# Rows of the last eight modes split in six and two; Z of the last two as four partial products; x of the first tile summed in PSUM

## The chip, the cores and the metric

The kernel runs on one core of one Trainium2 chip. The metric is the device time in microseconds (us), the median of three runs. All names of lines below (L432 and so on) are lines of the kernel before; the same lines of the changed kernel have higher numbers.

## The reference

Linear attention is followed by a spectral mixing block. With `phi(t) = elu(t) + 1`, batch 8, 8 heads, 576 positions and a head width of 64:

```
kv  = einsum('bhsd,bhse->bhde', phi(k), v);  z = phi(k).sum(axis=2)
x   = einsum('bhsd,bhde->bhse', phi(q), kv) / (einsum('bhsd,bhd->bhs', phi(q), z)[..., None] + 1e-6)
x   = x.transpose(0, 2, 1, 3).reshape(8, 576, 512)
X   = rfft(x, axis=1)[:, :64]                       # 64 modes are kept
Y   = einsum('bmd,mde->bme', X, w_r + 1j * w_i)     # one 512 x 512 complex matrix for each mode
u   = x + irfft(Y, n=576, axis=1)
out = u + relu(u @ w_ch)                            # 8 x 576 x 512 float32
```

The weights `w_r` and `w_i` are 64 matrices each of 512 x 512 in float32, together 134 MB to be read.

## The kernel before

**Stages.** First, q, k and v are loaded and x is formed and transformed by a product with DFT columns. Then `mode_pair(p)` runs for p = 0 to 30, two modes at a time: POOL issues the DMAs of the weights (`w_load`, L117, two buffers that alternate), TensorE multiplies the spectrum with them (`product`, L432, into `P`), `evacuate` copies `P` to SBUF, and `picks` (L455) adds the four column groups and puts Y, with the channels on partitions, into the PSUM tile `yt_ps`. While the weights of a pair land, TensorE does other work out of the list `work` (attention rows, the channel product of x, inverse transforms of the modes that are done), dealt out by `slots`, and `keep_warm(n)` (L419) adds n products of 128x512 whose result nobody reads. The inverse transform is a product too: `inv_sb` holds its rows, and `inv2_sb` and `lead_sb` hold such rows picked and reordered for the late modes.

**The last pair of modes.** `last_pair()` loads mode 62 and mode 63 in pieces (`w_load_last`, L129). Mode 62 goes through `product`, `evacuate` and `picks`. Mode 63 is computed turned, with the weights as the stationary operand (L513, `y_last`, 32 products of 128x16), in five pieces `PIECES` as the last weights land, eight or four products a piece, and one `keep_warm` product after some. The result of the eight last modes (56 to 63) is in `Y8` (128 channels x 4 x 8 modes x 16): seven modes are copied there by L506, the last one by L519.

**The tail.** From `Y8` two things are needed, with the 128 rows (mode, part, batch) on partitions: the rows themselves (half 0 of the tile `last`, by four transposes, L932) and Z, which is the rows times `w_ch` (half 1 of `last`, by products with `wch16`, L938). L933 and L934 copy the transposed rows to `last`, L943 copies Z. Two DMAs (L947, one on SP's queue, one on POOL's) send `last` to `YZ_all`, where the later batches read it. The output tiles are 128 x 512; two of them, a pair n, share `accs[n]` of two PSUM banks. For a tile the order is: `channels` (L800, the product of x with `w_ch`, kept in `E0`, is put in PSUM), `add_inverse(n, 1)` (L760, the inverse transform of Z is added), relu on ScalarE (L958 for single tiles, L810 later), `add_inverse(n, 0)` (the inverse transform of the rows is added), and one sum on VectorE that adds x out of SBUF (L962 for one tile, L834 for a pair), and then a store on SP's queue. The first eight tiles (pairs 0 to 3, batches 0 and 1) read `last` itself; later ones read `YZ_all`. The first tile is done apart: the inverse transform of its rows goes to `y0` (L944), VectorE adds it to x (L945), and one instruction does relu and sum (L973).

**What sets the order.** Nearly all instructions are pinned to the order of the program on their engine; each engine takes its own in that order. Semaphore waits follow from the tiles that are read and written, and from the reuse of buffers: `psW` has the tags "P" (two buffers), "yt" (one) and "zl" (one, the target of `keep_warm`), and after its release the pool `psT1` takes its banks for the accumulators of pairs 2 and 3.

Of the kernel before, what the change touches and what calls it, by code (L numbers as in the profile page):

```python
# [10 lines left out]
F32 = mybir.dt.float32  # L11
F16 = mybir.dt.float16
# [31 lines left out]
def kernel(  # L44
# [22 lines left out]
    NL = 8  # L67
    NE = NM - NL
    NF = NM // 2

    fwd_np, inv_np, pick_np = _dft_consts(S, NM)
    id16_dr = nc.inline_tensor(np.eye(128, dtype=np.float16), name="ident16")
# [343 lines left out]
    def keep_warm(n: int):  # L416

        for _ in range(n):
            pin(nc.tensor.matmul(last_ps[0], id16, wch16[:, 0, :]))  # L419
# [67 lines left out]
    def last_pair():  # L487
        xl = ystage.tile([128, NDL, 2 * B], BF16, name="xl")
        for h in range(2):
            src = xt_v[:, (2 * h + 1) * NDC : (2 * h + 2) * NDC, :, :, LAST]  # L490
            pin(
                nc.vector.tensor_copy(
                    out=xl[:, h * NDC : h * NDC + NDC], in_=src.rearrange("p c t b -> p c (t b)")
                )
            )
        w = w_get(LAST)
        kk = NM - 2
        work_slot(LAST, "start")
        P = psW.tile([128, D], F32, tag="P", bufs=2, name=f"P{kk}")
        for dc in range(NDL):  # L500
            n = 32 if dc < NDC else 2 * B
            product(P, xt_cols(dc, kk, n), n, w, dc, NDL)
        st = evacuate(kk, P)
        work_slot(LAST, "mid")
        picks(kk, st, 1)
        pin(nc.vector.tensor_copy(out=Y8[:, :, 0 : NL - 1, :], in_=yt_ps[:, :, 0 : NL - 1, :]))  # L506
        keep_warm(3)
        y_last = psW.tile([128, NDC, 2 * B], F32, tag="P", bufs=2, name="y_last")
        for piece in PIECES:
            for dc in range(piece.start, piece.stop):  # L510
                for ec in range(NDC):
                    pin(
                        nc.tensor.matmul(  # L513
                            y_last[:, ec, :], w[:, NDL + dc, ec * 128 : ec * 128 + 128], xl[:, dc, :],
                            start=(dc == 0 and ec == 0), stop=(dc == NDL - 1), skip_group_check=True,
                        )
                    )
            keep_warm(WARM[piece.stop])
        nc.vector.tensor_copy(out=Y8[:, :, NL - 1, :], in_=y_last)  # L519
# [18 lines left out]
    inv2_sb = ystage.tile([128, S], F16, name="inv2_sb")  # L538
    N_LEAD = 2
    lead_sb = [ystage.tile([128, S], F16, name=f"lead{b}_sb") for b in range(N_LEAD)]  # L540
    nc.sync.dma_start(out=inv_sb, in_=inv_dr.ap())
    YE_T = ystage.tile([128, NDC, NF, 2 * B], F16, name="YE_T")
    YL = [ystage.tile([128, NDC // 2, 2, 2 * NL, NF // NL, B], F16, name="YL0")]
# [62 lines left out]

    last_ps = []

    sel = sW.tile([128, 1 + N_LEAD, 128], F16, tag="rows", bufs=1, name="row_sel")

    def row_sets():
        pin(nc.vector.memset(sel, 0.0))
        for h in range(2):
            for g in range(NF // NL):
                r0 = 2 * NF + 2 * NL * ((g - 1) % (NF // NL))
                pin(
                    nc.vector.tensor_copy(
                        out=sel[:, 0, h * 64 + g : h * 64 + 64 : NF // NL], in_=id16[:, r0 : r0 + 2 * NL]
                    )
                )  # L620
        for b in range(N_LEAD):
            pin(nc.vector.tensor_copy(out=sel[:, 1 + b, b:128:B], in_=id16[:, 2 * NE : 128]))

    def row_set(i: int):
        dst = ([inv2_sb] + lead_sb)[i]
        for cols in (slice(0, 512), slice(512, S)):
# [157 lines left out]
    def on_bank(n: int, banks: set, ins):  # L784
        pin(ins)
        for other, theirs in users.setdefault(n, []):
            if not banks & theirs:
                tc.declare_no_dep(ins.ins, other.ins, reason="the other bank of the pair")
        users[n].append((ins, banks))
    accs: dict[int, object] = {}  # L790

    def channels(n: int, tiles_of=(0, 1)):
        if n not in accs:
            accs[n] = acc_pools[n % 4 // 2].tile([128, 2, D], F32, tag="acc", bufs=2, name=f"acc{n}")
        for i in tiles_of:
            t = pairs[n][i]
            for cols, src in e0_parts(t):
                on_bank(
                    n, {i},
                    nc.tensor.matmul(  # L800
                        accs[n][:, i, cols], id16, src, start=(cols.start == 0), stop=False,
                        skip_group_check=True,
                    ),
                )
# [94 lines left out]
    rows_work = [row_sets] + [lambda i=i: row_set(i) for i in range(1 + N_LEAD)]  # L899
# [8 lines left out]
    for p in range(n_early, LAST):  # L908
        mode_pair(p)
    assert not work  # L910
    psB.release()
# [3 lines left out]
    slots[LAST, "start"] = slots[LAST, "mid"] = N_PRE  # L915
    for n in range(N_PRE):
        work += [lambda n=n: channels(n), lambda n=n: first_rows(n)]
    last_pair()


    last = sW.tile([128, 2, D], F16, tag="rows", bufs=1, name="last")
    z1_ps = psW.tile([128, NDC, 8, 2 * B], F32, tag="yt", bufs=1, name="z1l")
    y_ps = [
        psW.tile([128, NDC, 128], F16, tag="P", bufs=2, name=f"ypl{h}")[:, 0 : NDC // 2] for h in range(2)
    ]
    y0 = psW.tile([128, D], F32, tag="P", bufs=2, name="y0l")
    last_ps.append(z1_ps.rearrange("p c m n -> p (c m n)"))
    rows = [Y8[:, ec].rearrange("p m n -> p (m n)") for ec in range(NDC)]
    hw = D // 2
    COLS = [slice(h * hw, h * hw + hw) for h in range(2)]  # L930
    for ec in range(NDC):
        pin(nc.tensor.transpose(y_ps[ec // 2][:, ec % 2, :], rows[ec], id16))  # L932
    pin(nc.scalar.copy(out=last[:, 0, COLS[0]], in_=y_ps[0].rearrange("p c r -> p (c r)")))  # L933
    pin(nc.vector.tensor_copy(out=last[:, 0, COLS[1]], in_=y_ps[1].rearrange("p c r -> p (c r)")))  # L934
    for h in range(2):
        for ec in range(NDC):
            pin(
                nc.tensor.matmul(  # L938
                    last_ps[h][:, 0:hw], rows[ec], wch16[:, ec, COLS[h]],
                    start=(ec == 0), stop=(ec == NDC - 1),  # L940
                )
            )
        pin(nc.scalar.copy(out=last[:, 1, COLS[h]], in_=last_ps[h][:, 0:hw]))  # L943
    pin(nc.tensor.matmul(y0, lead_sb[0][:, rows_of(0)], last[:, 0, :]))  # L944
    pin(nc.vector.tensor_tensor(out=x_of(0), in0=y0, in1=x_of(0), op=ALU.add))  # L945
    for h, eng in enumerate((nc.sync, nc.gpsimd)):
        eng.dma_start(  # L947
            out=YZ_all[64 * h : 64 * h + 64 : NF // NL].rearrange("r b z d -> r b (z d)"),
            in_=last.rearrange("p z d -> p (z d)"),
        )  # L950
    psW.release()
    acc_pools.append(
        tc.alloc_tile_pool(name="psT1", bufs=1, space=PSUM, side="left", reuse_waits="tile")
    )

    def relu(n: int, i: int):
        a = accs[n][:, i]
        on_bank(n, {i}, nc.scalar.activation(out=a, in_=a, func=AF.Relu))  # L958
# [8 lines left out]
        add_inverse(n, 1, (i,))  # L967
        relu(n, i)

    add_inverse(0, 1, (1, 0))  # L970
    on_bank(
        0, {0},
        nc.vector.scalar_tensor_tensor(  # L973
# [51 lines left out]
```

## Time and profile before

| | us |
|---|---|
| median of three runs (lowest, highest) | 421.56 (421.41, 422.10) |
| span of the profiled execution, first to last instruction | 419.4 |
| what lies around the span, median less span | 2.2 |
| TensorE busy in the span | 317.2 (76%) |
| VectorE busy in the span | 231.3 (55%) |
| ScalarE busy in the span | 154.2 (37%) |
| weights' queue (software DMA), share of the 16 DMA engines | 93.4% |
| last DVE instruction of mode 63's result (L519) ends at | 388.45 |
| first output store is issued at | 391.59 |
| last output store is issued at | 414.13 |

The runs are of whole executions; the profile is one execution, and its own time is the span and the 2.2 us around it. All places in time below are microseconds from the start of the span. A line of the timeline gives the start, the time until the group's last instruction ends, the engine, the line of the source, the operation, what it writes and reads, the shape and the count, and in brackets how long the engine stood idle before it and for whom. A line of the chain of waits gives the start, the length and what was at work. The ends of matmuls are modelled, and they overlap: ten of them that are listed with 2.32 us begin 0.215 us after each other.

### The profile page before, as it was taken

Reading aid. Unit: us, or ns where it says so; the run is one execution under the profiler, and the core shown is the slowest. Engines: PE = TensorE matmul, PEld = TensorE weight load, DVE = VectorE, ACT = ScalarE, POOL = GpSimd, SP = SyncE. Lnnn points to the kernel's source line nnn. Section 1 sums busy time; section 2 is a strip of 40 time slices with the busy share of each in tenths; the row PEclk is TensorE's granted clock in tenths of the full one; section 3 lists DMA queues with packets and bytes.
Section 4 is the critical chain, followed back from the end, with each engine's and each line's share of the span. In section 5 each row is a group of like instructions: output and inputs, shape, how many; then the busy total and the mean of one; then the engine's idle time right before and its main releaser. Section 6 shows DMA issues by size and latency. Waiting matters only on the chain.

```text
span 419.4 us, 7466 instructions
## 1 busy us (share of the span) xinstructions
PE 317.2 (76%) x3143; PEld 164.4 (39%) x3143; DVE 231.3 (55%) x509; ACT 154.2 (37%) x253; POOL 57.4 (14%) x100
## 2 busy tenths in 40 slices
PE   0369998999617875676767686988798877998993
PEld 0257776877301332222222233433343332453421
DVE  4588899785314563463645353464456443522794
ACT  4677798854201011000000233334253432330783
POOL 4222224210011211111111111111111111130000
PEclk9999999579855658665655599899899997899998
DMA  8999999999999999999999999999999999998698
GB/s 217 211 212 216 210 222 203 228 206 223 217 223 208 218 220 209 220 217 212 220 214 213 223 213 214 223 210 216 220 209 219 217 214 219 216 209 166 235 391 328
DMA packets 17073, 93.17 MB, mean 222 GB/s; under 512 B 2112, under 2 KB 3024, under 8 KB 12880
## 3 DMA queue, kind: packets, MB, share of 16 engines
q0 software_dynamic: 12496, 81.48, 93.4%
q1 hardware_dynamic: 4544, 11.22, 7.2%
q8 instruction: 24, 0.39, 0.3%
q14 instruction: 9, 0.07, 0.0%
HBM read 163.93 MB, written 9.44 MB: 413 GB/s over the span
## 4 chain that ended last, share of the span: by engine, by line
DMA 64%; PE 23%; DVE 4%; POOL 3%; ACT 3%; issue 2%; DVEq 0%; ACTq 0%; POOLq 0%
DMA w<-in_moe_w_i_dram 53%; DMA pick_sb<-row_pick 8%; PE P L432 6%; DMA k<-in_k_dram 3%; PE acc L760 3%; PE kvp L257 3%; PE acc L800 2%; POOL w L117 2%; PE z L726 1%; DVE x L293 1%; ACT ke L208 1%; PE xf L355 1%; PE zl L419 1%; PE qTp L237 1%; PE num L163 1%
## 5 line engine op out<-in xcount | busy, mean ns | idle before, releaser
L432 PE MATMUL P<-w,xz 128*32 128x512 bf16 x496 | 42.6, 475 | 37.6 <-DMA w<-in_moe_w_i_dram 35.4
L419 PE MATMUL zl<-wch,id 128*128 128x512 f16 x185 | 58.2, 466 | 0.0
L449 ACT CAST ys<-P 128x512 f16<-128x512 f32 x15 | 8.8, 586 | 132.4 <-PE P L432 132.4
L117 POOL DMA_DIRECT2D w<-in_moe_w_r_dram x31 | 17.3, 559 | 246.4 <-PE P L432 211.8
L447 DVE CAST ys<-P 128x512 f16<-128x512 f32 x17 | 11.8, 692 | 51.0 <-PE P L432 51.0
L706 PE MATMUL eps<-wch,xTw 128*128 128x512 f16 x144 | 39.3, 399 | 0.0
L432 PEld LDWEIGHTS <-xz 128*32 128x32 bf16 x496 | 12.6, 108 | 63.3 <-DMA w<-in_moe_w_i_dram 40.3
L163 PEld LDWEIGHTS <-qT 64*128 64x128 f16 (+1 forms) x640 | 22.6, 122 | 29.6 <-issue 15.6
L689 ACT CAST x16w<-x_main 128x512 f16<-128x512 f32 x32 | 19.8, 618 | 37.8 <-DVE x_main L687 37.8
L687 DVE TENSOR_TENSOR x_main<-ya,x_main 128x512 f32<-128x512 f32 x32 | 22.0, 689 | 16.5 <-PE ya L683 16.3
L257 PE MATMUL kvp<-vpad,ke 32*128 32x130 f16 x576 | 24.3, 263 | 8.9 <-ACT qT L244 6.1
L442 DVE COPY xz<-xt_c 64x256 bf16<-64x256 bf16 x62 | 23.0, 371 | 10.9 <-PE P L432 10.0
L419 PEld LDWEIGHTS <-id 128*128 128x128 f16 x185 | 18.9, 112 | 25.6 <-issue 14.3
L714 ACT CAST E<-eps 128x512 f16<-128x512 f32 (+1 forms) x40 | 21.2, 540 | 17.7 <-PE eps L706 17.7
L257 PEld LDWEIGHTS <-ke 32*128 32x128 f16 x576 | 22.3, 116 | 10.6 <-issue 8.6
L163 PE MATMUL nw<-kv_sb,qT 64*128 64x65 f16 (+1 forms) x320 | 18.2, 231 | 9.8 <-DVE x_tail L650 4.7
L237 PE MATMUL qTp<-id,qe 128*128 128x128 f16 x144 | 15.1, 289 | 10.6 <-DVE qe L221 9.5
L293 DVE TENSOR_TENSOR x<-num,rd 128x512 f16<-128x512 f32 x32 | 22.1, 692 | 1.1
L650 DVE TENSOR_TENSOR x_main<-nw,rd 128x256 f32<-128x256 f32 x32 | 11.2, 416 | 18.8 <-PE nw L163 18.8
L455 PE MATMUL yt<-pick_sb,ys 128*128 128x32 f16 (+1 forms) x128 | 8.8, 185 | 16.7 <-DMA pick_sb<-row_pick 9.4
L698 DVE COPY xTw<-xTp 128x512 f16<-128x512 f16 x36 | 15.0, 416 | 10.3 <-PE xTp L696 10.3
L208 ACT ACTIVATE qe<-q 128x1152 f16<-128x1152 f16 (+1 forms) x16 | 17.9, 1157 | 7.2 <-DMA q<-in_q_dram 7.1
(118 smaller groups left out, 507.5 us busy)
## 6 DMA issues: line engine op xcount, KB each, us to landing
w<-in_moe_w_r_dram POOLq DMA_DIRECT2D x31, 1024.0 KB, 13.2
w<-in_moe_w_i_dram POOLq DMA_DIRECT2D x31, 1024.0 KB, 17.5
out_dram<-x_main SPq DMA_DIRECT2D x12, 512.0 KB, 3.6
k<-in_k_dram POOLq DMA_DIRECT2D x8, 576.0 KB, 12.9
v<-in_v_dram POOLq DMA_DIRECT2D x8, 576.0 KB, 14.3
q<-in_q_dram POOLq DMA_DIRECT2D x7, 576.0 KB, 12.6
out_dram<-x_main SPq DMA_DIRECT2D x8, 256.0 KB, 4.0
q<-in_q_dram SPq DMA_DIRECT2D x2, 576.0 KB, 4.5
```

Source lines behind the costliest of these rows:

```text
L117: nc.gpsimd.dma_start(out=w_in[p][half::2], in_=two.rearrange("g (r dc) e -> (g r) dc e", dc=NDW))
L163: mm = nc.tensor.matmul(num[hpo][orow, c0 : c0 + 65], qT[rows, hpp, h2, cols], kv_sb[rows, hpp, h2, :])
L208: pin(nc.scalar.activation(out=ev[:, c], in_=heads(nm, b, c), func=AF.Exp))
L257: nc.tensor.matmul(kv_ps[:, h2, 0:130], phi["k", b][r0 : r0 + 32, j // NJ, j % NJ].rearrange("p o d -> p (o d)"), vp[r0 : r0 + 32, :, j, 0 ...
L293: nc.vector.tensor_tensor(out=dst.rearrange("p (o c d) -> p o c d", o=2, c=4), in0=nv[:, :, :, 0:64], in1=rden.unsqueeze(3).broadcast_to([ ...
L419: pin(nc.tensor.matmul(last_ps[0], id16, wch16[:, 0, :]))
L432: nc.tensor.matmul(P[c : c + n, :], x, w[:, dc, :], start=(dc < NDC), stop=(dc >= n_dc - NDC), tile_position=(0, c), skip_group_check=True,)
L442: pin(nc.vector.tensor_copy(out=xz[p % 2][HALVES[h], :, h, :], in_=src))
L687: pin(nc.vector.tensor_tensor(out=x, in0=acc, in1=x, op=ALU.add))
L689: pin(nc.scalar.copy(out=x16w[t], in_=x))
L706: nc.tensor.matmul(e_ps, xT[:, c, :], wch16[:, c, :], start=(c == 0), stop=(c == NDC - 1))
L714: pin(nc.scalar.copy(out=dst, in_=e_ps[:, cols]))
```

## The change

1. `rows_done()`, ahead of mode 62's products: six modes of `Y8` (`NA = 6`, 96 rows) are copied, transposed (`ya`), and multiplied with `w_ch` (`za`); the results go to rows 0 to 95 of `last`, the first by ScalarE, the second by VectorE.
2. `done_sums(n)` for n = 0 and 1: the inverse transform of these 96 rows of Z is added to the accumulators of the first four tiles, as part of the list `work` in mode 62's slots.
3. L506 copies one mode instead of seven. `first_sum()` takes the place of `keep_warm(3)`: a product of the identity in float32 (`id32`) with x of the first tile, in float32, starts the accumulation `y0`.
4. After the last weights: the two last modes (32 rows, at partitions 96 to 127) are transposed in four products. Z of these 32 rows is formed as four partial products, one for each chunk of 128 channels, each in 32 partitions of one bank (`tile_position=(0, c)`); one copy on VectorE takes all four to SBUF (`parts0`), and `part_sum` adds them in the inverse transform by `quarter_sb`, whose 128 rows hold the 32 rows of the inverse four times. ScalarE copies the finished `y0` over x of the first tile.
5. After the four `part_sum` and three relus, Z of the 32 rows is formed again in full (`full_z`), copied to `last` in two halves by ScalarE and VectorE, and then come the two DMAs from `last` to `YZ_all`.
6. `row_sets` and `row_set` make `quarter_sb` (one more VectorE copy, one product, one ScalarE copy) in the middle of the kernel.

```diff
@@ last_pair
         kk = NM - 2
+        rows_done()
         work_slot(LAST, "start")
...
         picks(kk, st, 1)
-        pin(nc.vector.tensor_copy(out=Y8[:, :, 0 : NL - 1, :], in_=yt_ps[:, :, 0 : NL - 1, :]))
-        keep_warm(3)
+        pin(nc.vector.tensor_copy(out=Y8[:, :, NA, :], in_=yt_ps[:, :, NA, :]))
+        first_sum()
...
+    def rows_done():
+        pin(nc.vector.tensor_copy(out=id32, in_=id16))
+        pin(nc.vector.tensor_copy(out=Y8[:, :, 0:NA, :], in_=yt_ps[:, :, 0:NA, :]))
+        ya = psW.tile([128, NDC, 128], F16, tag="P", bufs=2, name="ya_ps")
+        for ec in range(NDC):
+            pin(nc.tensor.transpose(ya[0:RA, ec, :], done_rows(ec, 0, NA), id16))
+        pin(nc.scalar.copy(out=last[0:RA, 0, :], in_=ya[0:RA].rearrange("p c r -> p (c r)")))
+        za = psW.tile([128, D], F32, tag="P", bufs=2, name="za_ps")
+        for ec in range(NDC):
+            pin(nc.tensor.matmul(za[0:RA, :], done_rows(ec, 0, NA), wch16[:, ec, :], ...))
+        pin(nc.vector.tensor_copy(out=last[0:RA, 1, :], in_=za[0:RA, :]))
+    def done_sums(n: int):
+        for i, t in enumerate(pairs[n]):
+            on_bank(n, {i}, nc.tensor.matmul(accs[n][:, i], lead_sb[0][0:RA, rows_of(t, BASE[0])], last[0:RA, 1, :], ...))
+    def first_sum():
+        y0 = psW.tile([128, D], F32, tag="yt", bufs=1, name="y0l")
+        pin(nc.tensor.matmul(y0, id32, x_of(0), start=True, stop=False))
...
     for n in range(N_PRE):
-        work += [lambda n=n: channels(n), lambda n=n: first_rows(n)]
+        work += [lambda n=n: channels(n), lambda n=n: first_rows(n), lambda n=n: done_sums(n)]
...
     for ec in range(NDC):
-        pin(nc.tensor.transpose(y_ps[ec // 2][:, ec % 2, :], rows[ec], id16))
-    pin(nc.scalar.copy(out=last[:, 0, COLS[0]], in_=y_ps[0].rearrange("p c r -> p (c r)")))
-    pin(nc.vector.tensor_copy(out=last[:, 0, COLS[1]], in_=y_ps[1].rearrange("p c r -> p (c r)")))
-    for h in range(2):
-        for ec in range(NDC):
-            pin(nc.tensor.matmul(last_ps[h][:, 0:hw], rows[ec], wch16[:, ec, COLS[h]], ...))
-        pin(nc.scalar.copy(out=last[:, 1, COLS[h]], in_=last_ps[h][:, 0:hw]))
-    pin(nc.tensor.matmul(y0, lead_sb[0][:, rows_of(0)], last[:, 0, :]))
-    pin(nc.vector.tensor_tensor(out=x_of(0), in0=y0, in1=x_of(0), op=ALU.add))
-...
+        pin(nc.tensor.transpose(y_ps[lastr, ec, :], done_rows(ec, NA, NL), id16))
+    for ec in range(NDC):
+        c = 32 * ec
+        pin(nc.tensor.matmul(z_ps[c : c + 32, :], done_rows(ec, NA, NL), wch16[:, ec, :], tile_position=(0, c)))
+    pin(nc.scalar.copy(out=last[lastr, 0, COLS[0]], in_=y_ps[lastr, 0:2].rearrange("p c r -> p (c r)")))
+    pin(nc.vector.tensor_copy(out=last[lastr, 0, COLS[1]], in_=y_ps[lastr, 2:4].rearrange("p c r -> p (c r)")))
+    pin(nc.vector.tensor_copy(out=parts0, in_=z_ps))
+    pin(nc.tensor.matmul(y0, lead_sb[0][:, rows_of(0)], last[:, 0, :], start=False, stop=True))
+    pin(nc.scalar.copy(out=x_of(0), in_=y0))
...
-    add_inverse(0, 1, (1, 0))
+    part_sum(0, 0)
...
     store(0, 1)
-    relu(0, 1)
-    for i in range(2):
-        add_inverse(1, 1, (i,))
-        relu(1, i)
+    for n, i in ((0, 1), (1, 0), (1, 1)):
+        part_sum(n, i)
+        relu(n, i)
+    full_z(range(NDC))
+    pin(nc.scalar.copy(out=last[lastr, 1, COLS[0]], in_=zf_ps[lastr, COLS[0]]))
+    pin(nc.vector.tensor_copy(out=last[lastr, 1, COLS[1]], in_=zf_ps[lastr, COLS[1]]))
+    for h, eng in enumerate((nc.sync, nc.gpsimd)):
+        eng.dma_start(
+            out=YZ_all[64 * h : 64 * h + 64 : NF // NL].rearrange("r b z d -> r b (z d)"),
+            in_=last.rearrange("p z d -> p (z d)"),
+        )
+    psW.release()
```

More of the change, by code (lines that the diff above doesn't have):

```diff
@@ L69 @@
     NF = NM // 2
+    NA = NL - 2
+    RA = 2 * B * NA
     fwd_np, inv_np, pick_np = _dft_consts(S, NM)
@@ L540 @@
     lead_sb = [ystage.tile([128, S], F16, name=f"lead{b}_sb") for b in range(N_LEAD)]
+    quarter_sb = ystage.tile([128, NJJ * 128], F16, name="quarter_sb")
     nc.sync.dma_start(out=inv_sb, in_=inv_dr.ap())
@@ L607 @@
     last_ps = []
-    sel = sW.tile([128, 1 + N_LEAD, 128], F16, tag="rows", bufs=1, name="row_sel")
+    sel = sW.tile([128, 2 + N_LEAD, 128], F16, tag="rows", bufs=1, name="row_sel")
     def row_sets():
@@ L622, in row_sets @@
             pin(nc.vector.tensor_copy(out=sel[:, 1 + b, b:128:B], in_=id16[:, 2 * NE : 128]))
+        pin(
+            nc.vector.tensor_copy(
+                out=sel[:, 1 + N_LEAD, 0:128:B].rearrange("p (c k) -> p c k", c=NDC),
+                in_=id16[:, 2 * (NM - 2) : 128].unsqueeze(1).broadcast_to([128, NDC, 4]),
+            )
+        )
     def row_set(i: int):
-        dst = ([inv2_sb] + lead_sb)[i]
-        for cols in (slice(0, 512), slice(512, S)):
+        dst = ([inv2_sb] + lead_sb + [quarter_sb])[i]
+        for cols in (slice(0, 512), slice(512, S))[: 1 if i > N_LEAD else 2]:
             r_ps = bank(f"rows{i}_{cols.start}")[:, 0 : cols.stop - cols.start]
@@ L897, in first_rows @@
             )
-    rows_work = [row_sets] + [lambda i=i: row_set(i) for i in range(1 + N_LEAD)]
+    rows_work = [row_sets] + [lambda i=i: row_set(i) for i in range(2 + N_LEAD)]
     work[:0] = [lambda t=t: attention_rows(t) for t in tiles[:8]] + rows_work + [
@@ L910, with done_rows @@
     assert not work
+    last = sW.tile([128, 2, D], F16, tag="rows", bufs=1, name="last")
+    parts0 = sW.tile([128, D], F16, tag="xTw", bufs=2, name="z_parts")
+    id32 = sW.tile([128, 2, 128], F32, tag="x16w", bufs=2, name="id32")[:, 0, :]
+    hw = D // 2
+    COLS = [slice(h * hw, h * hw + hw) for h in range(2)]
+    y0 = None
+    def done_rows(ec: int, lo: int, hi: int):
+        return Y8[:, ec, lo:hi].rearrange("p m n -> p (m n)")
+    def rows_done():
[7 more added lines that the diff above has]
+        for ec in range(NDC):
+            pin(
+                nc.tensor.matmul(
+                    za[0:RA, :], done_rows(ec, 0, NA), wch16[:, ec, :],
+                    start=(ec == 0), stop=(ec == NDC - 1),
+                )
+            )
+        pin(nc.vector.tensor_copy(out=last[0:RA, 1, :], in_=za[0:RA, :]))
+    def done_sums(n: int):
+        for i, t in enumerate(pairs[n]):
+            on_bank(
+                n, {i},
+                nc.tensor.matmul(
+                    accs[n][:, i], lead_sb[0][0:RA, rows_of(t, BASE[0])], last[0:RA, 1, :],
+                    start=False, stop=False, skip_group_check=True,
+                ),
+            )
+    def first_sum():
+        nonlocal y0
+        y0 = psW.tile([128, D], F32, tag="yt", bufs=1, name="y0l")
+        pin(nc.tensor.matmul(y0, id32, x_of(0), start=True, stop=False))
     psB.release()
@@ L914 @@
     )
-    slots[LAST, "start"] = slots[LAST, "mid"] = N_PRE
     for n in range(N_PRE):
-        work += [lambda n=n: channels(n), lambda n=n: first_rows(n)]
+        work += [lambda n=n: channels(n), lambda n=n: first_rows(n), lambda n=n: done_sums(n)]
+    slots[LAST, "start"] = slots[LAST, "mid"] = len(work) // 2
     last_pair()
[L921 to L930, printed above, removed]
-    for ec in range(NDC):
-        pin(nc.tensor.transpose(y_ps[ec // 2][:, ec % 2, :], rows[ec], id16))
-    pin(nc.scalar.copy(out=last[:, 0, COLS[0]], in_=y_ps[0].rearrange("p c r -> p (c r)")))
-    pin(nc.vector.tensor_copy(out=last[:, 0, COLS[1]], in_=y_ps[1].rearrange("p c r -> p (c r)")))
@@ L935 @@
-    for h in range(2):
-        for ec in range(NDC):
+    y_ps = psW.tile([128, NDC, 128], F16, tag="P", bufs=2, name="ypl")
+    z_ps = last_ps[0]
+    lastr = slice(RA, 128)
+    for ec in range(NDC):
+        pin(nc.tensor.transpose(y_ps[lastr, ec, :], done_rows(ec, NA, NL), id16))
+    for ec in range(NDC):
+        c = 32 * ec
+        pin(
+            nc.tensor.matmul(
+                z_ps[c : c + 32, :], done_rows(ec, NA, NL), wch16[:, ec, :], tile_position=(0, c)
+            )
+        )
@@ new lines, with part_sum @@
+    pin(nc.scalar.copy(out=last[lastr, 0, COLS[0]], in_=y_ps[lastr, 0:2].rearrange("p c r -> p (c r)")))
+    pin(
+        nc.vector.tensor_copy(
+            out=last[lastr, 0, COLS[1]], in_=y_ps[lastr, 2:4].rearrange("p c r -> p (c r)")
+        )
+    )
+    pin(nc.vector.tensor_copy(out=parts0, in_=z_ps))
+    def part_sum(n: int, i: int):
+        t = pairs[n][i]
+        on_bank(
+            n, {i},
+            nc.tensor.matmul(
+                accs[n][:, i], quarter_sb[:, rows_of(t, BASE[0])], parts0,
+                start=False, stop=True, skip_group_check=True,
+            ),
+        )
@@ L937, with full_z @@
+    zf_ps = psW.tile([128, D], F32, tag="P", bufs=2, name="zf_ps")
+    def full_z(ecs):
+        for ec in ecs:
             pin(
                 nc.tensor.matmul(
-                    last_ps[h][:, 0:hw], rows[ec], wch16[:, ec, COLS[h]],
+                    zf_ps[lastr, :], done_rows(ec, NA, NL), wch16[:, ec, :],
                     start=(ec == 0), stop=(ec == NDC - 1),
@@ L942 @@
             )
-        pin(nc.scalar.copy(out=last[:, 1, COLS[h]], in_=last_ps[h][:, 0:hw]))
[L944 to L954, printed above, removed]
+    pin(nc.tensor.matmul(y0, lead_sb[0][:, rows_of(0)], last[:, 0, :], start=False, stop=True))
+    pin(nc.scalar.copy(out=x_of(0), in_=y0))
     def relu(n: int, i: int):
@@ L977 @@
     store(0, 1)
-    relu(0, 1)
-    for i in range(2):
-        add_inverse(1, 1, (i,))
-        relu(1, i)
+    for n, i in ((0, 1), (1, 0), (1, 1)):
[8 more added lines that the diff above has]
+            in_=last.rearrange("p z d -> p (z d)"),
+        )
+    psW.release()
+    acc_pools.append(
+        tc.alloc_tile_pool(name="psT1", bufs=1, space=PSUM, side="left", reuse_waits="tile")
+    )
     singles = [(n, i) for n in range(4) for i in range(2)][1:]
```

## The prediction

> **What bounds the kernel now.** I read the chain of waits first. Until 386.6 us it is the transfer of the weights, and no work of TensorE, VectorE or ScalarE that fits beneath it costs time. The end of the chain:
>
> ```profile
> 372.98 13.65 DMA w<-in_moe_w_i_dram
> ...
> 386.67 0.36 PE y_last L513 x8
> ...
> 388.23 0.24 DVE Y L519
> ...
> 388.51 0.40 PE ypl L932 x4
> ```
>
> The reader should see that the weights give way to TensorE only in the last two microseconds. Next comes the timeline of TensorE around this place. It asks how much room there is ahead of the last weights.
>
> ```profile
> 380.06 2.32 PE L419 MATMUL zl<-wch,id 128*128 128x512 f16 x10
> 382.21 0.59 PE L800 MATMUL acc<-E,id 128*128 128x512 f16 x2
> ...
> 385.09 0.81 PE L419 MATMUL zl<-wch,id 128*128 128x512 f16 x3
> 386.14 0.35 PE L513 MATMUL y_last<-xl,w 128*128 128x16 bf16 x8 [0.24 <-DMA w<-in_moe_w_i_dram]
> 386.67 0.36 PE L513 MATMUL y_last<-xl,w 128*128 128x16 bf16 x8 [0.19 <-DMA w<-in_moe_w_i_dram]
> ```
>
> From 380.06 to 385.9 TensorE is never idle; its waits are 0.24 and 0.19 us. The trace's semaphore updates have the five pieces complete at 386.01, 386.63, 387.21, 387.56 and 387.88. So only about 1 us of work can be put ahead of the pieces before TensorE runs behind the last of them.
>
> Then the tail, by the timeline of VectorE and the table of stretches (us, busy time and count of each engine, clock, DMA share, GB/s):
>
> ```profile
> 388.94 0.29 DVE L934 COPY last<-ypl 128x256 f16<-128x256 f16 x1 [0.49 <-PE ypl L932]
> 390.03 0.69 DVE L945 TENSOR_TENSOR x_main<-y0l,x_main 128x512 f32<-128x512 f32 x1 [0.80 <-PE y0l L944]
> 390.87 0.69 DVE L973 SCALAR_TENSOR_TENSOR x_main<-acc,x_main 128x512 f32<-128x512 f32 x1
> ...
> 402.04 9.65 DVE L834 TENSOR_TENSOR x_main<-acc,x_main 128x1024 f32<-128x1024 f32 x8
> ```
>
> ```profile
> 397.10:414.20 17.10, 15.27 (x86) 3.95 (x84) 16.78 (x14) 13.66 (x26) 0.00 (x0) 1.00 1.00 395
> ```
>
> From 390 on VectorE hardly rests (16.78 of 17.10 us after 397.1), and the stores behind it keep the DMA engines full. A later start of this train moves the end by as much, since neither can hurry.
>
> **The change, part one: ahead of the last weights.** Call T the end of L519, 388.45 before. TensorE leaves the ten `keep_warm` at 382.21; they stay. The new copies on VectorE (`id32`, six modes) stand beneath these ten. Added: four transposes and four 128x512 products; the four pairs of the same shape earlier (z L726, yp L736) take 0.87 and 0.25, so 1.12. Added: `done_sums`, four products of 128x512 by 0.215, 0.86. The copies of `ya` (ScalarE, 0.59 as L449) and `za` (VectorE, 0.69 as L447) lie beneath `channels(0)` and `first_rows(0)`, 1.08 long; were that cover gone, 0.7 would be added. The last picks end their issue at 385.09 + 1.98 = 387.07. `first_sum` now waits for L506's successor, because `y0` takes the buffer of `yt_ps`: from the last pick to the copy 0.18, the copy 0.22 (as L519, the same size), 0.06 to TensorE. So the float32 product starts at 387.53, and all 32 products of mode 63 are queued behind this wait. The removed three `keep_warm` had no such wait.
>
> The price of the float32 product is in no row. Its lower bound is one f16 product, 0.22. Its operands have twice the bytes on both sides, thus 2 x 2 f16 products, 0.86; with four uncovered weight loads of 0.11 (L419's PEld row) it is 1.31, the upper bound. I take 0.86, the value without exposed loads, since the loads of the f16 row are covered.
>
> The page FP8 and Floating Point Precision of the Trainium skill (TensorE Precision Notes) has true FP32 in four passes, and a reduced reading that truncates: by the first the sum stays, by the second it is 0.64 smaller; no row here tells which.
>
> TensorE thus reaches mode 63 at 388.39, after every piece has landed. At its own pace the three groups of eight and two `keep_warm` between them take 1.06 (0.21 each), and from the fourth group to T 0.62 (before: 387.69 to 388.45, less 0.14 of waiting). T becomes 390.07: **later by 1.6** (1.0 to 2.1 by the float32 product's bounds).
>
> **Part two: from T to the train of sums.** Times from T; before, the sum of the first tile began at +2.42, the next (L962) at +3.25. The built program's list of waits shows that in the changed kernel VectorE's copy of the transposed rows waits for ScalarE's copy of their other half; before, the two ran side by side. Transposes ready +0.46; ScalarE's copy 0.49 to 0.86 (0.37, L933); VectorE's 0.90 to 1.19 (0.29, L934); `parts0` behind it on the same engine 1.15 to 1.84 (0.69 as L447, 128x512 f32 to f16); `y0` 1.24 to 1.62, ScalarE's copy to x 1.66 to 2.25 (0.59); `part_sum` of the first tile 1.89 to 2.27; relu and sum from 2.31 to 3.00. First store 0.1 earlier from T: the removed x add (0.69) and two Z copies are paid back by `parts0` and the serial copies.
>
> Here a rule speaks against the partial products. Four products in 32 columns each cost little: L432's groups of four start 0.22 apart, against 0.87 for the eight half products of before (388.74 to 389.61). But `parts0` takes the full 0.69.
>
> The page TensorEngine Tiling (Array Packing), PSUM Bottleneck, says that tiling speeds TensorE but not the PSUM evacuation, and advises both engines for it; had the copy shrunk fourfold too, the first sum would come 0.5 earlier and the total be 3.9.
>
> Then Z in full. TensorE issues the other three `part_sum` and `full_z` until 3.61; ScalarE does three relus (0.54 each) from 2.52 and copies its half of Z only behind them, 4.14 to 4.51. VectorE's half waits for that copy, and by length lies between L519 (0.22 for 64) and L506 (0.63 for 448): 0.43, so 4.55 to 4.98. VectorE takes instructions in order, so the second tile's sum, ready at 4.0, stands behind it until 4.94 (before 3.25: 1.7 late). The bank of pair 2 is free only after the same copy, so TensorE's next products wait until 5.02, and the third sum begins at 5.88 (before 3.90: 2.0 late).
>
> Last, the DMAs to `YZ_all` start at 5.0 (before 1.76), and land 3.7 and 4.3 later by the DMA view: 8.7 and 9.3. Pair 4 wants the first at 7.82, and behind that wait stands the product for the seventh tile's sum: it begins at 9.53 instead of 6.73. **Later by 2.8**. From there the train has the same work as before.
>
> **The rest.** `quarter_sb` (a VectorE copy, a product, a ScalarE copy) lies under the weights' DMA in the middle, where the chain of waits has one wait of 17.5 us for weights after the other: 0, and 1.1 if it had no cover (0.29, 0.22, 0.59). DMA issues of the weights wait for products of pair 29, which don't move.
>
> **Sum.** 1.6 + 2.8 = 4.4. The profiled execution becomes 419.4 + 4.4 = 423.8; around the span lie 2.2, as before; on the median, 421.56 + 4.4 = **426.0**.
>
> **The rivals.** *A, the forecast*: 425.0 to 427.2. The ends are the float32 bounds (-0.6, +0.5), a landing of the `YZ_all` DMAs by 0.6 later, beside the first store, and a small backlog of stores, up to 0.3, that the hole would empty. 0.74.
>
> *B, the transfers pace the tail*: output stores land 3.1 to 4.2 us after their issue, the longest at the end, so a backlog builds; if the first store's time alone decided, the shift would be 1.6 - 0.1, **423.1**. Against it: the DMA view after 397 has a slice of 212 GB/s beside ones of 384 and 391, a hole with no backlog left, behind the place of the delay. 0.12.
>
> *C, faster*: the earlier first store leads the train. Place: between T and the first store. If the wait of VectorE's copy for ScalarE's costs nothing, the rows are ready at 0.86, `parts0` ends at 1.44 and the first sum begins at 1.95, 0.47 earlier: **421.1**. It decides only if TensorE reaches mode 63 by 386.77 (now 388.39), that is with 1.6 us of the added work free, and if Z's copies are ready by 3.25. 0.05.
>
> *D, worse*: the clock falls to half, as in some slices of the page, in the new holes of TensorE (1 us at 4.0, 0.9 at 7.8); the eleven products from 5.02 to 7.6 would then take 2.4 longer: **428.4**. Against it: the granted clock is 1.00 in every stretch from 378 to 414.2, and the holes are short. 0.09.
>
> **Numbers.** The range must leave out no more than 0.2: 422.9 to 427.6 takes in A and B and part of D. Faster by over 0.2% (0.84 us, about what a measurement of this kernel can tell): 0.04, the larger part of C; within 0.2%: 0.03, its rest and a little of B; slower: 0.93.
>
> **What would show it.** In the changed profile the first products of mode 63 start near 388.4 without waiting for a DMA; the float32 product is a row of 0.2 to 1.3; T is near 390.1; VectorE idles some 1.5 us between the first and the second tile's sums; the sum of the seventh tile begins near T + 9.5, with TensorE waiting for `YZ_all`. If T stays near 388.5, part one is wrong; if VectorE's train is unbroken after the first sum, part two is.

## The result, and the profile after

The changed kernel takes 426.19 us in the median (425.46 to 426.61, four runs), against 421.57 for the kernel before: a ratio of 1.0107, with a 95% interval of 1.0093 to 1.0121 (the ratios are estimated from all executions, so they need not be the quotient of two medians). It is slower by 4.6 us; 426.0 was forecast. All times and ratios here are of executions in the same, faster state of the chip; one execution of a run below, at 431.48 us, fell into a slower state and is left out. Its profiled span is 424.5 us, 5.1 longer than the 419.4 of before.

The lines that answer to TensorE's stretch ahead of the last weights, from the timeline of TensorE in the changed kernel (start, length, engine, line, operation, shape, count, and in brackets the idle time before):

```profile
380.96 2.32 PE L421 MATMUL zl<-wch,id 128*128 128x512 f16 x10
383.11 0.39 PE L937 MATMUL ya_ps<-id,Y 128*96 128x128 f16 x4
383.34 1.03 PE L942 MATMUL za_ps<-wch,Y 128*96 128x512 f16 x4
...
388.54 1.13 PE L962 MATMUL y0l<-x_main,id 128*128 128x512 f32 x2 [0.32 <-DVE Y L509]
389.50 0.55 PE L516 MATMUL y_last<-xl,w 128*128 128x16 bf16 x16
```

Before, the first products of mode 63 began at 386.14 after a wait for the weights. Now they begin at 389.50, wait for nothing, and sixteen run in one go: the trace's semaphore updates have the last piece complete at 388.00, before TensorE came to the first one. The wait of 0.32 for L509 and the float32 product stand in front of them, as forecast. The float32 product is shown as two records, and its place in TensorE's queue, from its start to that of the next product, is 0.96 long (388.54 to 389.50).

The same stage on VectorE, from its timeline in the changed kernel:

```profile
390.93 0.22 DVE L522 CAST Y<-y_last 128x64 f16<-128x64 f32 x1 [2.44 <-PE y_last L516]
392.03 0.30 DVE L988 COPY last<-ypl 32x256 f16<-32x256 f16 x1 [0.89 <-ACT last L986]
392.36 0.69 DVE L992 CAST z_parts<-zl 128x512 f16<-128x512 f32 x1
393.60 0.69 DVE L1035 SCALAR_TENSOR_TENSOR x_main<-acc,x_main 128x512 f32<-128x512 f32 x1 [0.54 <-PE acc L998]
395.77 0.43 DVE L1045 CAST last<-zf_ps 32x256 f16<-32x256 f32 x1 [1.48 <-ACT last L1044]
396.23 0.69 DVE L1024 TENSOR_TENSOR x_main<-acc,x_main 128x512 f32<-128x512 f32 x1
397.10 2.63 DVE L1024 TENSOR_TENSOR x_main<-acc,x_main 128x512 f32<-128x512 f32 x4 [0.18 <-PE acc L770]
400.25 0.69 DVE L1024 TENSOR_TENSOR x_main<-acc,x_main 128x512 f32<-128x512 f32 x1 [0.52 <-PE acc L770]
```

T, the end of the copy of mode 63's result, is 391.15 (before 388.45). VectorE waits for ScalarE's half of the rows (0.89); before, the two halves stood in two PSUM tiles and were copied side by side, now they stand in one. VectorE then stands idle for 1.48 between the first tile's sum and the copy of Z; the sums of the other tiles are queued behind that copy. Later, by the table of stretches, the train of sums has its old pace:

```profile
402.19:419.20 17.01, 15.28 (x86) 3.95 (x84) 16.80 (x14) 13.68 (x26) 0.00 (x0) 1.00 1.01 400
```

VectorE is busy for 16.80 of 17.01 us (before 16.78 of 17.10) with the same 14 sums. All that is lost is lost ahead of 402.19. Measured from T, the profiles before and after give: first tile's sum at +2.42 and +2.45; second at +3.25 and +5.08; seventh at +6.73 and +9.10; end of the last sum at +25.65 and +28.05. So the 5.1 us of the profile are 2.7 ahead of T and 2.4 behind it.

Of the 2.7, 0.9 lie still further ahead: the products of the last full pair (modes 60 and 61) began at 379.00 instead of 378.10. From the timelines of TensorE, before and after:

```profile
378.10 1.05 PE L432 MATMUL P<-w,xz 128*32 128x512 bf16 x16 [0.27 <-DMA w<-in_moe_w_i_dram]
379.00 1.05 PE L434 MATMUL P<-w,xz 128*32 128x512 bf16 x16
```

The span from those products to T went from 10.35 to 12.15, by 1.8. The median of the runs grew by less than the profiled span, 4.6 against 5.1, because the profiled execution before was a quick one. In every execution on record the time exceeds the span by about 1.8 us; the 2.2 us given above sets a median against the span of another execution. The span of 419.4 thus stands for about 421.2 us, 0.4 under the median, while the profiled execution after, 426.27 us, is close to its median. The 0.9 is looked at below.

### The profile page after: what moved, and what is told of

Its sections match the earlier page's. It is cut to its first block, busy times and chain, and to the rows that moved or that the text cites. A ratio compares the mean times of both kernels' runs of the same rounds, so it can differ in the third digit from the quotient of the medians.

```text
span 424.5 us, 7500 instructions
## 1 busy us (share of the span) xinstructions
PE 321.0 (76%) x3155; PEld 164.3 (39%) x3155; DVE 232.7 (55%) x514; ACT 155.4 (37%) x255; POOL 57.5 (14%) x100
## 4 chain that ended last, share of the span: by engine, by line
DMA 56%; PE 27%; DVE 7%; ACT 3%; issue 3%; POOL 2%; DVEq 0%; ACTq 0%; POOLq 0%
DMA w<-in_moe_w_i_dram 44%; DMA pick_sb<-row_pick 8%; PE P L434 6%; PE zl L421 4%; DMA k<-in_k_dram 3%; PE acc L770 2%; PE kvp L259 2%; PE z L736 2%; PE acc L810 2%; PE eps L716 2%; DVE x L295 1%; POOL w L119 1%; ACT ke L210 1%; DMA YZ_all<-last 1%; PE yb L755 1%
## 5 line engine op out<-in xcount | busy, mean ns | idle before, releaser
L434 PE MATMUL P<-w,xz 128*32 128x512 bf16 x496 | 45.7, 505 | 35.8 <-DMA w<-in_moe_w_i_dram 33.4
L239 PE MATMUL qTp<-id,qe 128*128 128x128 f16 x144 | 14.1, 276 | 11.5 <-DVE qe L223 9.5
L165 PE MATMUL num<-kv_sb,qT 64*128 64x65 f16 (+1 forms) x320 | 16.5, 218 | 5.5 <-DVE x L295 3.2
```

The source lines that it names most:

```text
L165: mm = nc.tensor.matmul(num[hpo][orow, c0 : c0 + 65], qT[rows, hpp, h2, cols], kv_sb[rows, hpp, h2, :])
L434: nc.tensor.matmul(P[c : c + n, :], x, w[:, dc, :], start=(dc < NDC), stop=(dc >= n_dc - NDC), tile_position=(0, c), skip_group_check=True,)
```

## The experiments

The theory, as in the prediction: two delays in series. TensorE is given more work ahead of mode 63 than the weights leave room for, and Z in full, copied late, holds up VectorE's train and the copy to `YZ_all`. The rivals: the output transfers pace the tail, so that the time of the first store alone decides; work put ahead of the last weights is paid in full; the 0.9 us are an effect of the new rows in the middle.

**How much room there is ahead of mode 63.** Two runs put a dose of empty work into the kernel before.

```diff
-        keep_warm(3)
+        keep_warm(7)
```

> The kernel before with seven keep_warm products instead of three ahead of mode 63: 4 x 0.215 = 0.86 us more work on TensorE. Two-delay theory: there is about 1 us of room (385.74 to 386.77), so T moves by less than 0.1 and the time is 421.6. Rival 'any work put ahead of mode 63 is paid in full': 422.4.

Measured: 421.44 us, ratio 1.0001 (0.9991 to 1.0011); T is 388.50 in the profile, 0.05 later. TensorE reached mode 63 0.5 us later, at 386.65, and paid nothing.

```diff
-        keep_warm(3)
+        keep_warm(15)
```

> The kernel before with fifteen keep_warm products instead of three ahead of mode 63: 12 x 0.215 = 2.58 us more work on TensorE. Two-delay theory: 2.58 less the 1.03 of room, T later by 1.5, and the tail unchanged from T: 423.0 to 423.2. Rival 'the transfers pace the tail and swallow a later start': 421.6 to 422.2. Rival 'paid in full': 424.1.

Measured: 423.60 us, ratio 1.0048 (1.0030 to 1.0066). The timeline of TensorE in this run:

```profile
385.30 3.40 PE L419 MATMUL zl<-wch,id 128*128 128x512 f16 x15
388.53 0.55 PE L513 MATMUL y_last<-xl,w 128*128 128x16 bf16 x16
388.94 0.38 PE L419 MATMUL zl<-wch,id 128*128 128x512 f16 x1
```

Sixteen products in one go, as in the changed kernel: the weights lie ready. T is 390.18, later by 1.73 (0.2 of it because the last full pair began 0.2 later in this execution), and from T to the end of the last sum it is 25.64, as before. So a room of about 1 us is shown, and a later T is passed on whole: the transfers at the end swallow none of it. The two runs together are against the rival that work ahead of the last weights is paid in full (the dose of 0.86 was free), and this one against transfers that would swallow a later start.

**The middle of the kernel.** The quarter rows alone, in the kernel before.

```diff
...
-    rows_work = [row_sets] + [lambda i=i: row_set(i) for i in range(1 + N_LEAD)]
+    rows_work = [row_sets] + [lambda i=i: row_set(i) for i in range(2 + N_LEAD)]
```

> The kernel before with the making of the quarter rows alone (one VectorE copy, one product, one ScalarE copy in the middle of the kernel); nothing reads them. Two-delay theory: beneath the weights, 421.5, and the products of the last full pair begin near 378.1. Rival 'the 0.9 us by which the last full pair began later in the changed kernel's profile comes from this work': that pair begins near 379.0.

Measured: 421.38 us, ratio 0.9999 (0.9990 to 1.0008); the last full pair begins at 378.12. The rows cost nothing, and with them the pair begins in time, so they don't make the 0.9 us. (The median alone could not tell: a delay of 0.9 is nearly free in the kernel before, as the four added empty products show.)

**Part one, taken down in two ways.** First the ten empty products after the last full pair are left out of the changed kernel.

```diff
-    FILL = {**{p: 7 for p in range(5, 16)}, **{p: 7 for p in range(18, 27)}, 27: 7, 28: 10, 29: 12, 30: 10}
+    FILL = {**{p: 7 for p in range(5, 16)}, **{p: 7 for p in range(18, 27)}, 27: 7, 28: 10, 29: 12, 30: 0}
```

> The changed kernel without the ten keep_warm products that follow the last full pair. Two-delay theory: TensorE is late for mode 63 because of the work queued in front of it; 10 x 0.215 = 2.15 us go, of which about 0.65 stay as a wait for the copy of the six modes, so T (the end of the copy of mode 63's result) comes 1.5 us sooner and the time falls from 426.2 to about 424.7; the part after T is unchanged (the seventh tile's sum at T + 9.1). Rival 'transfers pace the tail': also 1.5 sooner. Rival 'the clock falls without the keep_warm': T is not sooner, 426 or more.

Measured: 425.45 us (424.03 to 425.85, three runs), ratio 1.0082 (1.0060 to 1.0105). In the profile T is 389.00, and the last sum ends at T + 28.04. From the last full pair to T it is 10.89, 1.26 less than in the changed kernel, where 1.5 was expected; TensorE stood idle 0.70 for the copy of the six modes, as reckoned. The gain in the median, 0.7, is small beside the spread of 1.8; the gain on T is what the profile shows. The rival of the falling clock is out for the profiled execution alone, the quickest of the three: the clock was 1.00 there. The others took 1.4 and 1.8 us longer, and a run below shows the clock at half in this very place.

Then the float32 product is left out, and VectorE adds `y0` to x as before.

```diff
-        pin(nc.vector.tensor_copy(out=id32, in_=id16))
...
-        pin(nc.tensor.matmul(y0, id32, x_of(0), start=True, stop=False))
...
-    pin(nc.tensor.matmul(y0, lead_sb[0][:, rows_of(0)], last[:, 0, :], start=False, stop=True))
-    pin(nc.scalar.copy(out=x_of(0), in_=y0))
+    pin(nc.tensor.matmul(y0, lead_sb[0][:, rows_of(0)], last[:, 0, :]))
+    pin(nc.vector.tensor_tensor(out=x_of(0), in0=y0, in1=x_of(0), op=ALU.add))
```

> The changed kernel without the float32 product: y0 starts with the rows, and VectorE adds it to x of the first tile, as before; no keep_warm stands in its place. Two-delay theory: the wait for the copy (0.32) and the product (0.96) leave TensorE's queue, T comes 1.3 us sooner; after T the sum of the first tile begins about 0.3 later, the second tile's sum does not move, since it hangs on ScalarE's relus and the copy of Z: 426.2 - 1.3 = 424.9. Rival 'the first store's time alone decides': 1.3 - 0.3 = 1.0 sooner, 425.2, and the seventh tile's sum is later from T.

Measured: 424.52 us, ratio 1.0081 (1.0058 to 1.0103). From the last full pair to T it is 10.73, 1.42 less. The first tile's sum is 0.16 later from T (+2.61), the second stays at +5.08 and the last sum's end at +28.07. A first store 0.16 later leaves all that follows from T where it was.

**Part two, undone.** Part one stays; Z of the 32 rows is formed once, in full, and sent out at once.

```diff
-    pin(nc.vector.tensor_copy(out=parts0, in_=z_ps))
+    pin(nc.scalar.copy(out=last[lastr, 1, :], in_=zf_ps[lastr, :]))
...
-                accs[n][:, i], quarter_sb[:, rows_of(t, BASE[0])], parts0,
+                accs[n][:, i], lead_sb[0][lastr, rows_of(t, BASE[0])], last[lastr, 1, :],
...
     pin(nc.scalar.copy(out=x_of(0), in_=y0))
+    for h, eng in enumerate((nc.sync, nc.gpsimd)):
+        eng.dma_start(
...
```

> Part one of the change kept, part two mostly undone: Z of the 32 rows is formed once, in full, copied by ScalarE at once, the DMAs to YZ_all go out ahead of the sums, and the sums of the first four tiles take 32 rows. Two-delay theory: the delay after T (2.4 in the profile, seventh tile at T + 9.1 instead of T + 6.7) falls to about 0.3, so about 2.1 less: 424.1. Rival 'the first store's time alone decides': the first sum begins 0.1 later from T, so no gain, 426.3. Rival 'the delay lies ahead of the tail altogether': no gain either.

Measured: 423.99 us, ratio 1.0056 (1.0041 to 1.0071). The first tile's sum is at T + 2.57, the second at +3.70, the seventh at +7.18, and the last sum's end at +26.10: 0.45 more than before, where the changed kernel has 2.40 more. The median falls by 2.2 us with a first sum that is 0.12 later, and the last sum's end is 1.95 nearer to T. The rival of the first store is out, and so is a delay that lies ahead of T altogether.

**Which of part two's waits is the last one.** The prediction had two: the hole on VectorE, and behind it the copy to `YZ_all`. Here the products of the full Z move ahead of the first tile's, and its two copies and the DMAs ahead of the second to fourth partial sums; the first store stays ahead of the copies and the DMAs.

```diff
+    full_z(range(NDC))
     pin(nc.tensor.matmul(y0, lead_sb[0][:, rows_of(0)], last[:, 0, :], start=False, stop=True))
...
     store(0, 1)
-    for n, i in ((0, 1), (1, 0), (1, 1)):
-        part_sum(n, i)
-        relu(n, i)
-    full_z(range(NDC))
     pin(nc.scalar.copy(out=last[lastr, 1, COLS[0]], in_=zf_ps[lastr, COLS[0]]))
     pin(nc.vector.tensor_copy(out=last[lastr, 1, COLS[1]], in_=zf_ps[lastr, COLS[1]]))
...
+    for n, i in ((0, 1), (1, 0), (1, 1)):
+        part_sum(n, i)
+        relu(n, i)
```

> The changed kernel with Z in full and its two copies moved ahead of the second to fourth partial sums, and the DMAs to YZ_all and the release of the banks with them; nothing is left out. Two-delay theory: VectorE's copy follows the first tile's sum without a hole, the second tile's sum begins at T + 3.7 instead of T + 5.1, the YZ_all DMAs go out at T + 3.5 instead of T + 5.1, the seventh tile's sum begins at about T + 7.8 instead of 9.1: 1.3 less, 424.9. Rival 'the first store's time alone decides': the first sum is 0.1 later, so 426.3.

Measured: 426.64 us, ratio 1.0122 (1.0107 to 1.0137): no gain at all, against the expectation of the theory. VectorE's timeline shows why; the hole has moved:

```profile
393.64 0.69 DVE L1036 SCALAR_TENSOR_TENSOR x_main<-acc,x_main 128x512 f32<-128x512 f32 x1 [0.62 <-ACT x_main L1017]
394.36 0.43 DVE L1042 CAST last<-zf_ps 32x256 f16<-32x256 f32 x1
395.06 3.28 DVE L1025 TENSOR_TENSOR x_main<-acc,x_main 128x512 f32<-128x512 f32 x5 [0.28 <-PE acc L770]
400.49 0.69 DVE L1025 TENSOR_TENSOR x_main<-acc,x_main 128x512 f32<-128x512 f32 x1 [2.14 <-PE acc L770]
```

The second tile's sum is 1.1 earlier (+3.95), but the seventh begins at +9.38 after 2.14 of idle time, with the product for it queued on TensorE behind the one that needs `YZ_all`. The copy on SP's queue went out at T + 3.76, 1.3 earlier than in the changed kernel, and landed later relative to its issue. The DMA view of this run:

```profile
YZ_all<-last SPq DMA_DIRECT2D x1, 256.0 KB, 4.8
YZ_all<-last POOLq DMA_DIRECT2D x1, 256.0 KB, 3.7
```

The rows of SP's copy in the changed kernel and in the kernel before:

```profile
YZ_all<-last SPq DMA_DIRECT2D x1, 256.0 KB, 3.2
YZ_all<-last SPq DMA_DIRECT2D x1, 256.0 KB, 3.7
```

So SP's copy took 3.2 us in the changed kernel and 3.7 before. It now follows the first store by 0.5 us (394.36 and 394.87), where it followed by 1.9 in the changed kernel and preceded it in the kernel before. That the store in front makes it slow was a guess at this point; the next run tries it by putting the copy ahead of the store.

```diff
+    full_z(range(NDC))
+    pin(nc.scalar.copy(out=last[lastr, 1, COLS[0]], in_=zf_ps[lastr, COLS[0]]))
+    pin(nc.vector.tensor_copy(out=last[lastr, 1, COLS[1]], in_=zf_ps[lastr, COLS[1]]))
+    for h, eng in enumerate((nc.sync, nc.gpsimd)):
+        eng.dma_start(
...
     pin(nc.tensor.matmul(y0, lead_sb[0][:, rows_of(0)], last[:, 0, :], start=False, stop=True))
...
```

> The changed kernel with Z in full, its two copies and the DMAs to YZ_all ahead of the first tile's sum and store. What the run with only the copies ahead of the other partial sums left open: whether its seventh tile was late because the YZ_all copy shared the DMA engines with the first store just ahead of it. Two-delay theory as amended (the YZ_all copy, not VectorE's hole, is the last to be late): YZ_all goes out at T + 2.3, lands by T + 6, the seventh tile's sum begins at about T + 7.1, the last sum ends at T + 26.0 instead of 28.05, 424.2. If the hole on VectorE alone mattered, or the tail were late for another reason, the end from T stays above 27.5 and the time above 425.7.

Measured: 424.31 us, ratio 1.0065 (1.0046 to 1.0083). VectorE's timeline:

```profile
393.71 0.69 DVE L1043 SCALAR_TENSOR_TENSOR x_main<-acc,x_main 128x512 f32<-128x512 f32 x1 [0.18 <-PE acc L998]
394.81 3.28 DVE L1032 TENSOR_TENSOR x_main<-acc,x_main 128x512 f32<-128x512 f32 x5 [0.41 <-PE acc L770]
398.30 0.69 DVE L1032 TENSOR_TENSOR x_main<-acc,x_main 128x512 f32<-128x512 f32 x1 [0.20 <-PE acc L770]
```

The DMA view of this run has, for SP's half:

```profile
YZ_all<-last SPq DMA_DIRECT2D x1, 256.0 KB, 3.6
```

The copy goes out at T + 2.42 and its halves land in 3.6 and 4.2; the seventh sum begins at T + 7.16 after 0.20 of idle time, and the last sum ends at T + 26.08. VectorE's hole is closed in both runs; they differ in when the copy goes out and in what goes ahead of it, and the end from T differs by 2.2 us. The earlier issue accounts for at most 1.34 of it. The remaining 0.9 then comes from the quicker landing of SP's copy (3.6 against 4.8), in the run where no store stands ahead of it.

The records of single packets in the two traces show where the 1.2 us of slower landing lie. With the store ahead, the store's packets on SP's queue are under way from 395.19 to 396.20, and the copy's from 396.40 to 398.3. The copy's first packet starts 1.53 after the issue, against 1.26 in the run without the store ahead (1.28 in the changed kernel, where the store is long done): 0.3 for the wait behind the store. The copy's packets then take 1.9 against 1.5: 0.4, in a stretch where the half on POOL's queue runs beside them from the start (its first packet comes 0.17 ahead of SP's, and in the other run 0.95 behind). The last 0.5 lie between the last packet and the landing (1.35 against 0.81). So the store in front accounts directly for about a quarter of the slower landing; why the two halves came together, and why the last landing was late, is open.

**Both repairs at once.** The run above, without the ten empty products.

> Both repairs at once: the ten keep_warm after the last full pair left out, and Z in full with its DMAs ahead of the first store. Two-delay theory: the delays add up without interaction. T near 389.0 (0.55 later than in the kernel before), the last sum's end at T + 26.1 (0.45 later): 421.5 + 1.0 = 422.5. If the two parts hide one another, the time is 423.5 or more, or 421.6 or less.

Measured: 422.70 us (ten runs, 422.16 to 423.86), ratio 1.0026 (1.0017 to 1.0036). The last sum ends at T + 26.08, as reckoned. In the profiled execution, the slowest of the ten, T was 390.59 and not 389.0: the granted clock was at half for 3.4 us from 380.7, in the stretch where the empty products had been. The table of stretches for this run, and for the run without the empty products alone (the last three numbers are the clock, the DMA share and GB/s):

```profile
380.70:384.10 3.40, 3.08 (x10) 1.37 (x10) 0.94 (x2) 0.58 (x1) 0.00 (x0) 0.50 1.02 206
380.70:384.10 3.40, 3.18 (x22) 1.31 (x22) 0.86 (x2) 0.58 (x1) 0.00 (x0) 1.00 1.01 199
```

TensorE starts 10 products there instead of 22, and from the last full pair to T it is 12.38 instead of 10.89. So in this execution the clock did fall where the empty products had been, as that rival has it; in the nine profiles with them it is at 1.00 there. That their absence is the cause is not shown by one profile of two. The median has most of the forecast gain. It stays slower than the kernel before, and no run here points to a version that beats it.

**The 0.9 us ahead of the last full pair.** In the profiles of the changed kernel and of the two runs that only moved Z, the pair began at 378.95 to 379.00, with the granted clock at half for 6.8 us from 354. The table of stretches of the changed kernel:

```profile
354.00:361.00 7.00, 6.48 (x22) 2.63 (x21) 3.99 (x8) 1.17 (x2) 0.00 (x0) 0.52 1.04 220
361.00:379.00 18.00, 18.00 (x127) 8.95 (x124) 6.56 (x13) 6.45 (x11) 4.92 (x10) 1.00 1.00 211
```

After the half clock TensorE is busy without a break until the pair, and reaches it when its weights already lie ready. In the kernel before the clock was at half from 352, and the pair began at 378.10; in the four runs of the changed kernel without the float32 product, with Z once, without the empty products and with both repairs it was full there, and the pair began at 378.11 to 378.21. But for the quarter rows, which the kernel before lacks, these kernels have the same program up to that pair, so the place of the half clock, and not the change, goes with the 0.9. Once TensorE is late for mode 63 anyway, such a delay is passed on to T; in the kernel before most of it would fall into the room of 1 us. How many executions of the changed kernel had it is not shown, since only one has a profile. Why the clock falls at one place or the other was not tried.

## Why the prediction was right

**The sum.** Forecast was 4.4 us, 1.6 ahead of T and 2.8 behind it; on the median it was 4.6. The mechanism held, but that the median was met to 0.2 is in part luck. The measured counterparts of the two terms are 1.8 and 2.4, together 4.2. The profile of the changed kernel has 0.9 more ahead of the last full pair, which no term of the prediction has, and the profile before is 0.4 short of its median: 4.2 + 0.9 - 0.4 = 4.7.

**Ahead of T.** Forecast 1.6, measured 1.8 from the last full pair to T. The steps came out: the room of 1 us (0.86 of empty work free, 2.58 paid with about 1.5 net of the pair's own start), the wait of L509's copy, the products of mode 63 at their own pace with all weights there. Two terms were too small, by 0.10 and 0.15. The float32 product takes 0.96, not 0.86, within the bounds of 0.22 and 1.31. And `done_sums` takes 1.01, not 0.86: its first product of 96 rows starts 0.31 after the product of 64 rows in front of it, and the second 0.24 to 0.25 after the first, not 0.215.

The page FP8 and Floating Point Precision of the Trainium skill (TensorE Precision Notes) names four passes for true FP32; 0.96 against 0.215 for the f16 product is 4.5 times, which speaks for these and not for the truncated reading.

**Behind T.** Forecast 2.8, measured 2.4. The first sum was forecast at +2.31 and came at +2.45, the second at +4.94 and came at +5.08, each 0.14 late by steps of less than 0.1 along the chain (`parts0` at +1.21 for +1.15, the first `part_sum` at +1.95 for +1.89). The seventh was forecast at +9.53 and came at +9.10. The mis-sized term is the copy to `YZ_all`: priced at 3.7 from the row of before, it landed in 3.2, and VectorE idled 0.52 for it. This was the luck of one execution as much as an error: the kernel before with more empty products, the same program in the tail, has SP's copy land in 3.5 (seven) and in 3.2 (fifteen).

The working names two waits, the hole on VectorE (third sum 2.0 late) and the copy behind it (seventh sum 2.8 late), and takes the later one, rightly. It does not say what closing the hole alone would give. The expectation of the later run did, 1.3 us, and was wrong: with the hole closed and the copy behind the first store the copy binds, and the end of the last sum stays at T + 28.3. With both gone the tail is T + 26.1.

**The rivals.** The transfers do not pace the tail by the first store: in the runs without the float32 product and with Z once, the first sum is later from T, and the end follows the train of sums, not the first store. The fast case needed mode 63 by 386.77; TensorE came at 389.50. The clock did not fall in the holes of the tail: it was 1.00 from 391.15 to 419.20.

The page TensorEngine Tiling (Array Packing), PSUM Bottleneck, warns that tiling does not speed the evacuation of PSUM. Here the four partial products start within 0.23 us (391.21 to 391.44), and their copy takes 0.69, as the rows of before said. Z formed once (first sum at +2.57, end at T + 26.10) is as good as Z in four parts with the copy to `YZ_all` put first (+2.58, T + 26.08): the partial products bring nothing here.

## What to carry to other kernels

Work that is moved ahead of the last transfer is free only up to the idle time that the in-order engine has there; count all of it, with the wait that its first instruction brings, against the time from the engine's last release to the landing of the last piece. At the start of a train that nothing later can hurry, look for the last of the waits and not for the first store: a result that goes through a DMA and comes back should be sent early, and ahead of stores that nobody waits for.

## What the runs showed of the hardware that was not expected

- A float32 product of 128x128 by 128x512 takes 0.96 us of TensorE's queue, in two records, against 0.215 for f16.
- The copy of 256 KB in SBUF on SP's queue landed 3.2 to 3.7 us after its issue in the ten profiles with no store close ahead, and in 4.8 in the one where a store of 256 KB had gone out 0.5 us before; about 0.3 of that is the wait for the store's packets.
- The half clock of TensorE comes at other places in executions of the same program text (from 354 in three profiles of the changed kernel and its variants, not at all there in four); in the stretch ahead of the last pair this went with 0.9 us.
